# Attention's operations in another order, two weight tiles rounded behind it, other shares of dense work per step

## The chip, the cores and the metric

The kernel runs on one core of one Trainium2 chip. The metric is the device time of one execution in microseconds (us), the median of several runs. The engines are named as in the profile: PE (TensorE), DVE (VectorE), ACT (ScalarE), POOL (GpSimd), SP (SyncE, whose queue issues most DMAs).

## The reference

Three parts follow one another, all in float32 (the weights arrive as 64-bit words and are rounded on the chip):

```python
def _attn_ref(q, k, v):                      # batch 4, 8 heads, 576 positions, 64 wide
    scores = scale * np.matmul(q, k.transpose(0, 1, 3, 2))
    ...
    mask = (rel >= 0) & (rel < window)       # window 128
    scores = np.where(mask, scores + bias[None], -1000000000.0)
    scores = scores - np.max(scores, axis=-1, keepdims=True)
    attn = np.exp(scores)
    attn = attn / (np.sum(attn, axis=-1, keepdims=True) + 1e-09)
    return np.matmul(attn, v).astype(np.float32)

def _moe_ref(x, w_gate, w_val, w_out):       # 2304 tokens, 512 -> 1536 -> 512
    gate = 1.0 / (1.0 + np.exp(-(x @ w_gate)))
    val = x @ w_val
    return (gate * val @ w_out).astype(np.float32)

def _moe2_ref(x, w1, w2, w3, w_out):         # 512 -> 1024 -> 1024 -> 512
    h = (x @ w1) * (x @ w2) @ w3
    return (h @ w_out).astype(np.float32)
```

## The kernel before, in words

The 2304 tokens are 18 tiles of 128, in five blocks of 2, 4, 4, 4 and 4 tiles (`TILES`). A float32 product is made of three fast products (`PASSES`): every operand is split into a high part, rounded by ACT (`act_copy`, line 80), and a remainder, high subtracted from the value, by DVE (`dve_lo`, line 83) or POOL (`pool_lo`, line 86).

**Attention** goes in steps. There are 20 units n, five blocks by four head pairs (block n // 4, pair n % 4), and in step n the kernel traces three stages of different units: `stage_p(n-2)`, `stage_pv(n-3)` and `stage_s(n)` (`ORDER` changes that for the first seven steps).

- `stage_s` makes the scores on PE (line 730), 16 matmuls; then for each half (two tiles) DVE merges the two key windows (copy_predicated, 738), scales and adds the bias (741), reduces to the negated maximum (747, and 751 rescales it); ACT takes four exps with row sums (754); DVE adds 1e-9 and takes the reciprocal of the sums (757, 758); POOL scales two of the four (762) and ACT the other two (764).
- `stage_p` transposes on PE (772) into two PSUM banks, ACT copies each out (tile cp, line 80) and POOL cuts each into two masked halves (776, 780).
- `stage_pv` multiplies with V on PE (795) into one bank; ACT takes the high part (xth) and DVE the remainder (xtl), which is the last reader of the bank.

The four PSUM banks of tag "mm" are shared by the transposes, by pv and by all dense products of this part.

**Dense work beside attention.** The first expert layer's slices come in groups: groups 0 and 1 have one slice of 128, the later ones two. `layer(group, block)` makes gate and value products (`gv`, line 360, two products per slice, four pieces each, a piece being three matmuls), tanh on ACT (377), gate times value on DVE (384), its high part on ACT (line 80, tile gt) and remainder on POOL (line 86). The down products (`down1`, line 401, four pieces with one bank each) of a layer are traced behind the next layer's gv; DVE copies or adds each bank into `acc` (409, 411). `READY` says at which step a layer may begin. Behind the stages of a step `fill(FILL[n])` traces pieces until a budget is used up: a piece of a 512-wide layer is booked at 680, of the 256-wide block 0 at 360, and the last piece may overshoot. `FILL` has a default of 4000.

**Weights.** `convert_next` rounds the next weight tile of a queue: ACT takes an absolute value (146), DVE runs six operations (`rounded`, 147 to 152), then the tile is either split (ACT 80, POOL 86) into a weight slot `wsl`, or written to DRAM (`early32`) by a DMA of SP's queue, to be read back later as plain float32. `CONVERT` says how many tiles a step rounds. In attention these are three tiles each of groups 0 and 1 (gate, value, out), and six of group 2 (slices 2 and 3) that go to `early32`: (2,0), (3,0), (2,1), (3,1), (2,2), (3,2), where the second number is 0 for gate, 1 for value, 2 for out. Behind attention the tiles of group 2 are read back and split, and the tiles of later groups and of the second expert layer are rounded, all beside dense products.

**What sets the order.** PE's order in attention is the order of tracing (`manual_schedule`). Every other engine's order is fixed when the program is built, by a scheduler that takes the ready instruction of the best rank first; the rank is the place in the trace, moved ahead by `high_priority(offset=...)` of a positive offset and back by a negative one. On the chip each engine then runs its list strictly in order. Before the change attention's own operations carry no offset, dense evacuations have `SOONER` (150) and the rounding of weights has minus `LATER` (300).

Of the kernel before, what the change touches and what calls it, by code (L numbers as in the profile page):

```python
# [9 lines left out]
F32 = mybir.dt.float32  # L10
# [3 lines left out]
AF = mybir.ActivationFunctionType  # L14
ALU = mybir.AluOpType
AX = mybir.AxisListType
# [3 lines left out]
P = 128  # L20
# [10 lines left out]
PASSES = ((0, 0), (0, 1), (1, 0))  # L31
LATER = 300
SOONER = 150
FILL = {5: 0.0, 6: 1400.0, 7: 1400.0, 8: 0.0, 9: 0.0, 10: 2700.0, 11: 2700.0}
FULL = 4000.0

LAST_ORDER = (4, 0, 1, 2, 3)
# [19 lines left out]
def attn_moe_kernel(  # L57
# [14 lines left out]
    nc = tc.nc  # L72
# [6 lines left out]
    def act_copy(dst, src):  # L79
        return nc.scalar.activation(dst, src, AF.Copy)  # L80

    def dve_lo(dst, src, hi):
        nc.vector.tensor_tensor(dst, src, hi.bitcast(F32), ALU.subtract)  # L83

    def pool_lo(dst, src, hi):
        nc.gpsimd.tensor_tensor(dst, src, hi.bitcast(F32), ALU.subtract)  # L86
# [23 lines left out]


    spool = capool = None
    staged = {}
    rings = {"raw": 2, "raw32": 0, "ca": 2}
    held = {"raw": 0, "raw32": 0}
    queue = []
# [60 lines left out]
    groups = [(0,), (1,)] + [tuple(range(i, i + GF)) for i in range(GF, NF + NM, GF)]  # L177
# [116 lines left out]
    early = [it for it in fold_src if it[0][0] == "o2" or it[0][1] in W3_AHEAD]  # L294
# [2 lines left out]
    early += [((i, c), (w1, w2)[c][i - NF]) for i in groups[NF // GF + 2] for c in range(2)]  # L297
    early += [it for it in fold_src if it[0][0] == "w3" and it[0][1] in W3_LATER]
    late_n = len(early)
    early += [((i, c), (w_gate, w_val, w_out)[c][i]) for c in range(3) for i in groups[2]]  # L300
    early32 = dpool.tile([P * len(early), DM], F32, name="early32")
    ahead = {key: early32[i * P : (i + 1) * P, :] for i, (key, _) in enumerate(early)}
    ahead_items = [(("ahead", *key), src, None) for key, src in early]
# [45 lines left out]
    def gv(grp, blk, xs):  # L349

        pss = {}
        w = cols(blk)
        ns = w / 2.4 + 13.3

        def product(i, s):
            full = gvpool.tile([P, TB], F32, tag=gvtag, name=f"gv{i}_{blk}_{s}", bufs=gvbufs)
            ps = pss[i, s] = full[:, 0:w]
            for kk in range(NK):
                for wp, xp in PASSES:
                    nc.tensor.matmul(  # L360
                        ps,
                        wsl[i][:, s, wp, kk * P : (kk + 1) * P],
                        xs[blk][xp][:, kk],
                        start=(kk == 0 and wp == 0 and xp == 0),
                        stop=(kk == NK - 1 and wp == 1),
                    )
# [12 lines left out]
        for i in grp:  # L379
            yield from product(i, 1)  # L380
            pr = g[i]
            t = m2.tile([P, 2, TB], F32R, tag="gt", name=f"gt{i}_{blk}", bufs=4)[:, :, 0:w]
            with tc.high_priority(offset=SOONER):
                nc.vector.scalar_tensor_tensor(pr, pr, 1.0, pss[i, 1], ALU.add, ALU.mult)  # L384
                act_copy(t[:, 0], pr)
                pool_lo(t[:, 1], pr, t[:, 0])
            ts.append(t)
        return ts
# [218 lines left out]
    def attention(actx, conv):  # L607
# [108 lines left out]
        def stage_s(n):  # L716
            pair, blk, nt, t0, back = where(n)
            s, ld = st[n], loads[n]
            x = s["sm"] = ap2.tile([P, 4, 2, P], F32, tag="sm", name=f"sm{n}", bufs=3)
            up = 4.0**pair  # L720
            pss = {}
            for tp in range(nt // 2):
                side = (tp + n) % 2

                ps = pss[tp] = spsum.tile([P, 2, 2, 2, P], F32, tag=f"s{side}", name=f"s{n}_{tp}")
                for u in range(2):
                    t = 2 * tp + u
                    for h in range(2):
                        r = slice(D * h, D * h + D)
                        nc.tensor.matmul(  # L730
                            ps[:, h, :, u], ld["q"][r, t * P : (t + 1) * P], ld["k"][r, t * P : (t + 2) * P],
                            start=True, stop=True, skip_group_check=True,
                        )
            for tp in range(nt // 2):
                ps = pss[tp]
                g = slice(2 * tp, 2 * tp + 2)

                nc.vector.copy_predicated(  # L738
                    ps[:, :, 1], mask.unsqueeze(1).unsqueeze(1).broadcast_to([P, 2, 2, P]), ps[:, :, 0]
                )  # L740
                nc.vector.scalar_tensor_tensor(  # L741
                    x[:, g].rearrange("p g u k -> p g (u k)"), ps[:, :, 1].rearrange("p g u k -> p g (u k)"),
                    0.125 * up, tabs[blk][:, g].rearrange("p g u k -> p g (u k)"), ALU.mult, ALU.add,
                )
                mn = ap2.tile([P, 4], F32, tag="mn", name=f"mn{n}_{tp}", bufs=4)
                su = ap2.tile([P, 4], F32, tag="su", name=f"su{n}_{tp}", bufs=4)
                s["dve"] = nc.vector.tensor_reduce(  # L747
                    mn, x[:, g].rearrange("p g u k -> p (g u) k"), axis=AX.X, op=ALU.max, negate=True
                )
                if pair:  # L750
                    nc.vector.tensor_scalar(mn, mn, 1.0 / up, None, ALU.mult)  # L751
                for j in range(4):
                    y = x[:, 2 * tp + j // 2, j % 2]
                    s["act"] = nc.scalar.activation(  # L754
                        y, y, AF.Exp, bias=mn[:, j : j + 1], scale=1.0 / up, accum_out=su[:, j : j + 1]
                    )
                nc.vector.tensor_scalar(su, su, 1e-9, None, ALU.add)
                s["rec"] = nc.vector.reciprocal(su, su)  # L758
                for j in range(4):
                    y = x[:, 2 * tp + j // 2, j % 2]  # L760
                    if j < 2:
                        nc.gpsimd.tensor_scalar(y, y, su[:, j : j + 1], 1.0, ALU.mult, ALU.mult)  # L762
                    else:
                        nc.scalar.activation(y, y, AF.Copy, scale=su[:, j : j + 1])

        def stage_p(n):
            pair, blk, nt, t0, back = where(n)
            s = st[n]
            for h in range(2):
                ps = gvpool.tile([P, 4, P], F32, tag="mm", name=f"pt{n}_{h}")  # L770
                for t in range(nt):
                    nc.tensor.transpose(ps[:, t], s["sm"][:, t // 2 * 2 + h, t % 2], ident)  # L772
                cp = ap2.tile([P, 4, 2, P], F32, tag="cp", name=f"cp{n}_{h}", bufs=4)
                own, prev = cp[:, 0:nt, 1], cp[:, 0:nt, 0]
                act_copy(own, ps[:, 0:nt])
                nc.gpsimd.affine_select(
                    out=prev, in_=own, compare_op=ALU.is_gt, fill=0.0, base=0,
                    pattern=[[0, nt], [-1, P]], channel_multiplier=1,
                )
                s["pool"] = nc.gpsimd.affine_select(  # L780
                    out=own, in_=own, compare_op=ALU.is_ge, fill=0.0, base=0,
                    pattern=[[0, nt], [1, P]], channel_multiplier=-1,
                )
                s["cp", h] = cp.rearrange("p t c k -> p (t c k)")

        def stage_pv(n):
            pair, blk, nt, t0, back = where(n)
            s = st[n]
            ps = gvpool.tile([P, TB], F32, tag="mm", name=f"pv{n}")[:, 0 : nt * P]
            for j in range(-back, nt):  # L790
                a, b = max(j, 0) * P, min(j + 2, nt) * P
                m0 = 0 if j < 0 else (2 * j + 1) * P
                for h in range(2):
                    c = slice(h * D, (h + 1) * D)
                    nc.tensor.matmul(  # L795
                        ps[c, a:b], loads[n]["v"][:, j + 1, c], s["cp", h][:, m0 : m0 + b - a],
                        start=j == -back, stop=j == nt - 1, skip_group_check=True,
                    )
            if pair == 0:
                xt.append(x_tile("xt", blk))  # L800
            x = xt[blk]
            act_copy(x[0][:, pair], ps)
            dve_lo(x[1][:, pair], ps, x[0][:, pair])

        def fill(budget):

# [5 lines left out]
                    budget -= cost  # L812


        CONVERT = {1: 1, 3: 1, 5: 1, 8: 1, 9: 1, 10: 1, 11: 1, 12: 1, 13: 2, 14: 2}

        READY = {5: ((0, 0),), 10: ((0, 1),), 12: ((1, 0),), 14: ((0, 2), (1, 1)), 18: ((0, 3), (1, 2))}
        ORDER = {
# [57 lines left out]
    accpools.append(ctx.enter_context(tc.tile_pool(name="acc0", bufs=1)))  # L876
    with ExitStack() as conv, ExitStack() as actx:
        attention(actx, conv)


    rings.update({"raw": 3, "raw32": 4, "ca": 4})
# [158 lines left out]
```

## Time and profile before

| | |
|---|---|
| median of 3 runs | 909.33 us (908.82 to 909.49) |
| the profiled execution | 909.88 us |
| its span, first to last instruction | 908.2 us |
| PE busy | 872.8 us (96%) |
| PE's weight loads busy | 715.5 us (79%) |
| DVE busy | 661.1 us (73%) |
| ACT busy | 351.8 us (39%) |
| POOL busy | 313.3 us (35%) |
| mean granted clock of PE | 0.991 |

The profiled execution takes 1.68 us more than its span. The busy shares are averages over a kernel of several stages; attention lies in the first 187 us or so, where PE has nearly all of its idle time, and behind it PE is busy without a gap worth naming. A wait is put down to the event that came last before the waiting instruction.

### The profile page before, as it was taken

How to read it: one execution, taken by the hardware profiler on the slowest of the kernel's cores; microseconds unless marked ns; L12 is line 12 of the kernel's file. 1: busy time of each engine (PE TensorE's matmuls, PEld its weight loads, DVE VectorE, ACT ScalarE, POOL GpSimd, SP SyncE). 2: the span in 40 equal slices, each digit the busy share in tenths (PEclk: the TensorE clock that was granted, in tenths of full speed). 3: DMA queues.
4: the chain of work that ended last, by engine and by line, in shares of the span. 5: the costliest groups of instructions: out<-in, count | busy, mean ns of one | idle time of the engine just before them, and what ended most of it. 6: DMA issues, size and time to landing. Idle time of an engine off the chain costs nothing.

```text
span 908.2 us, 12508 instructions
## 1 busy us (share of the span) xinstructions
PE 872.8 (96%) x4432; PEld 715.5 (79%) x4432; DVE 661.1 (73%) x1156; ACT 351.8 (39%) x853; POOL 313.3 (35%) x352
## 2 busy tenths in 40 slices
PE   6789888999999999999999999999999999999998
PEld 4456666788888888888888888878788888888886
DVE  5978899579996995896599954396547886733444
ACT  6878576633322322322332343243433333222120
POOL 4666655543312412422431211103643551112121
PEclk9989999999999999999999999999999999999999
DMA  5444443144451251152054440128524445654322
GB/s 194 154 145 144 139 165 126 36 151 131 131 184 44 85 189 41 47 175 92 23 184 153 140 140 1 70 84 289 206 95 172 175 185 185 225 197 158 117 92 93
DMA packets 40623, 121.67 MB, mean 134 GB/s; under 512 B 4464, under 2 KB 6512, under 8 KB 38512
## 3 DMA queue, kind: packets, MB, share of 16 engines
q1 hardware_dynamic: 39264, 106.05, 35.0%
q10 hardware_dynamic: 1296, 14.81, 3.9%
q8 instruction: 35, 0.57, 0.3%
q14 instruction: 28, 0.23, 0.1%
HBM read 88.34 MB, written 32.51 MB: 133 GB/s over the span
## 4 chain that ended last, share of the span: by engine, by line
PE 80%; DVE 12%; ACT 3%; POOL 2%; issue 2%; DMA 0%; SPq 0%; ACTq 0%; DVEq 0%; POOLq 0%
PE gv L360 30%; PE dn L401 14%; PE o L591 11%; PE pb L472 9%; PE pd L472 4%; PE w3o L321 3%; PE lone L565 3%; PE pc L472 2%; PE pv L795 2%; DVE s L738 2%; ACT sm L754 2%; DVE sm L741 2%; DVE mn L747 1%; PE pt L772 1%; PE s L730 1%
## 5 line engine op out<-in xcount | busy, mean ns | idle before, releaser
L360 PE MATMUL gv<-xth,wsl 128*128 128x512 f32 (+1 forms) x960 | 281.5, 371 | 1.3 <-DVE acc L409 0.8
L360 PEld LDWEIGHTS gv<-xth,wsl 128*128 128x128 f32 x960 | 175.9, 190 | 35.7 <-issue 3.0
L360 PE MATMUL gv<-xtl,wsl 128*128 128x512 f32 (+1 forms) x480 | 177.8, 370 | 0.7 <-DVE xtl L83 0.7
L86 POOL TENSOR_TENSOR gt<-g,gt 128x512 fp32r<-128x512 f32 (+1 forms) x60 | 79.3, 1324 | 250.8 <-ACT gt L80 250.8
L401 PE MATMUL dn<-gt,wsl 128*128 128x512 f32 (+1 forms) x720 | 155.0, 369 | 8.4 <-DVE xtl L83 5.2
L401 PEld LDWEIGHTS dn<-gt,wsl 128*128 128x128 f32 x720 | 125.7, 188 | 33.1 <-issue 6.1
L360 PEld LDWEIGHTS gv<-xtl,wsl 128*128 128x128 f32 x480 | 91.2, 190 | 15.9 <-DVE xtl L83 1.3
L472 PE MATMUL pb<-xf,forms 128*128 128x512 f32 x384 | 97.7, 391 | 0.0
L411 DVE TENSOR_TENSOR acc<-acc,dn 128x512 f32<-128x512 f32 (+1 forms) x120 | 72.8, 626 | 16.9 <-PE dn L401 16.8
L472 PEld LDWEIGHTS pb<-xf,forms 128*128 128x128 f32 x384 | 70.8, 188 | 14.9 <-ACT xb L80 0.5
L384 DVE SCALAR_TENSOR_TENSOR g<-g,gv 128x512 f32<-128x512 f32 (+1 forms) x60 | 37.5, 628 | 52.8 <-PE gv L360 51.2
L80 ACT ACTIVATE gt<-g 128x512 fp32r<-128x512 f32 (+1 forms) x60 | 35.1, 586 | 76.2 <-DVE g L384 76.2
L754 ACT ACTIVATE sm<-sm,mn 128x128 f32<-128x128 f32 x144 | 55.8, 390 | 18.1 <-DVE mn L751 12.7
L601 DVE TENSOR_TENSOR acc<-acc,o 128x512 f32<-128x512 f32 x54 | 36.8, 683 | 32.8 <-PE o L591 32.7
L86 POOL TENSOR_TENSOR tp<-x,tp 128x512 fp32r<-128x512 f32 x16 | 21.4, 1338 | 86.3 <-ACT tp L80 86.2
L472 PE MATMUL pd<-xf,forms 128*128 128x512 f32 x192 | 48.9, 390 | 0.8 <-DVE xb L515 0.8
L377 ACT ACTIVATE g<-gv 128x512 f32<-128x512 f32 (+1 forms) x60 | 32.7, 548 | 41.1 <-PE gv L360 37.2
L591 PE MATMUL o<-outw,tp 128*128 128x512 f32 x192 | 48.0, 390 | 0.3 <-POOL tp L86 0.3
L591 PE MATMUL o<-outw,tq 128*128 128x512 f32 x192 | 48.2, 389 | 0.0
L762 POOL TENSOR_SCALAR sm<-sm,su 128x128 f32<-128x128 f32 x72 | 32.1, 458 | 42.2 <-DVE su L758 28.9
L321 PE MATMUL w3o<-wo,w3s 128*128 128x512 f32 x192 | 44.4, 390 | 0.4 <-ACT w3s L80 0.4
L795 PE MATMUL pv<-cp,ldv 128*64 128x256 f32 (+1 forms) x352 | 40.8, 373 | 3.2 <-POOL cp L780 3.2
(797 smaller groups left out, 1455.5 us busy)
## 6 DMA issues: line engine op xcount, KB each, us to landing
formd<-forms ACTq DMA_DIRECT2D x8, 1792.0 KB, 7.3
outw<-outd SPq DMA_DIRECT2D x16, 512.0 KB, 5.5
forms<-formd SPq DMA_DIRECT2D x8, 1024.0 KB, 5.2
ldk<-in_k_dram SPq DMA_DIRECT2D x16, 320.0 KB, 3.9
ldv<-in_v_dram SPq DMA_DIRECT2D x16, 320.0 KB, 3.1
out_dram<-acc SPq DMA_DIRECT2D x18, 256.0 KB, 2.0
ldq<-in_q_dram SPq DMA_DIRECT2D x16, 256.0 KB, 4.3
outd<-w3o SPq DMA_DIRECT2D x8, 512.0 KB, 2.9
```

What stands on the lines that cost most here:

```text
L80: return nc.scalar.activation(dst, src, AF.Copy)
L86: nc.gpsimd.tensor_tensor(dst, src, hi.bitcast(F32), ALU.subtract)
L321: nc.tensor.matmul(acc2, w3s[u][:, wp, i * P : (i + 1) * P], wo2[kk][:, xp], start=(kk == 0 and wp == 0 and xp == 0), stop=(kk == NC2 - 1 ...
L360: nc.tensor.matmul(ps, wsl[i][:, s, wp, kk * P : (kk + 1) * P], xs[blk][xp][:, kk], start=(kk == 0 and wp == 0 and xp == 0), stop=(kk == N ...
L384: nc.vector.scalar_tensor_tensor(pr, pr, 1.0, pss[i, 1], ALU.add, ALU.mult)
L401: nc.tensor.matmul(ps, wsl[i][:, 2, wp, m * P : (m + 1) * P], t[:, xp], start=n == 0, stop=n == 3 * len(grp) - 1,)
L411: nc.vector.tensor_tensor(a, a, ps, ALU.add)
L472: nc.tensor.matmul(ps, forms[i][:, a, wp, kk * P : (kk + 1) * P], xf[n, j][:, xp, kk], start=first and kk == 0 and (wp, xp) == PASSES[0], ...
L591: nc.tensor.matmul(ps, ts2[n, i][blk][:, xp, tt * P : (tt + 1) * P], outw[i][:, wp], start=k == 0, stop=k == 3 * len(grp) - 1,)
L601: nc.vector.tensor_tensor(a, a, ps, ALU.add)
L754: s["act"] = nc.scalar.activation(y, y, AF.Exp, bias=mn[:, j : j + 1], scale=1.0 / up, accum_out=su[:, j : j + 1])
L795: nc.tensor.matmul(ps[c, a:b], loads[n]["v"][:, j + 1, c], s["cp", h][:, m0 : m0 + b - a], start=j == -back, stop=j == nt - 1, skip_group_ ...
```

## The change

Nothing is computed otherwise. The table `RANKS` gives offsets to kinds of operations; a kind that is not in it gets 0. In effect three kinds are moved: the remainders xtl by +200, the exps of block 3 (units 12 to 15) by +200, and, while attention runs, the high part of the gate product from +150 to -100. The row sums `su` get eight buffers in place of four. The two out tiles of group 2, (2,2) and (3,2), are no longer among the tiles rounded in attention and written to `early32`: they are read as 64-bit words and rounded behind it. `CONVERT` spreads the ten tiles left over other steps, and `FILL` has other budgets.

```diff
-FILL = {5: 0.0, 6: 1400.0, 7: 1400.0, 8: 0.0, 9: 0.0, 10: 2700.0, 11: 2700.0}
+RANKS = {"xtl": 200, "gact": -100, ("exp", 3): 200}
+FILL = {5: 0.0, 6: 1400.0, 7: 2800.0, 8: 0.0, 9: 0.0, 10: 3400.0, 11: 3400.0, 12: 2600.0, 13: 2600.0, 16: 6100.0, 17: 4700.0, 18: 3300.0, 19: 6800.0}
...
+    def ranked(kind, n):
+
+        return tc.high_priority(offset=RANKS.get((kind, n // 4), RANKS.get(kind, 0)))
+
...
+    attending = [True]
...
-    early += [((i, c), (w_gate, w_val, w_out)[c][i]) for c in range(3) for i in groups[2]]
+    early += [((i, c), (w_gate, w_val, w_out)[c][i]) for c in range(2) for i in groups[2]]
...
             with tc.high_priority(offset=SOONER):
                 nc.vector.scalar_tensor_tensor(pr, pr, 1.0, pss[i, 1], ALU.add, ALU.mult)
+            with tc.high_priority(offset=RANKS["gact"] if attending[0] else SOONER):
                 act_copy(t[:, 0], pr)
+            with tc.high_priority(offset=SOONER):
                 pool_lo(t[:, 1], pr, t[:, 0])
...
-                su = ap2.tile([P, 4], F32, tag="su", name=f"su{n}_{tp}", bufs=4)
...
+                su = ap2.tile([P, 4], F32, tag="su", name=f"su{n}_{tp}", bufs=8)
...
+                with ranked("exp", n):
+                    for j in range(4):
+                        y = x[:, 2 * tp + j // 2, j % 2]
+                        s["act"] = nc.scalar.activation(
...
-            act_copy(x[0][:, pair], ps)
-            dve_lo(x[1][:, pair], ps, x[0][:, pair])
+            with ranked("xth", n):
+                act_copy(x[0][:, pair], ps)
+            with ranked("xtl", n):
+                dve_lo(x[1][:, pair], ps, x[0][:, pair])
...
-        CONVERT = {1: 1, 3: 1, 5: 1, 8: 1, 9: 1, 10: 1, 11: 1, 12: 1, 13: 2, 14: 2}
+        CONVERT = {1: 1, 3: 2, 8: 1, 10: 1, 11: 1, 12: 1, 13: 1, 14: 1, 7: 1}
...
         attention(actx, conv)
+    attending[0] = False
```

The other operations of the stages (kinds "cp", "st", "red", "rec", "scale", "ptc", "sel", "xth") are wrapped in the same way, with an offset of 0.

## Rows read from the trace of the kernel before

**Rows 1.** The page: busy time, share of the span, instructions.

```profile
PE 872.8 (96%) x4432; PEld 715.5 (79%) x4432; DVE 661.1 (73%) x1156; ACT 351.8 (39%) x853; POOL 313.3 (35%) x352
```

**Rows 2.** Windows: length; PE, PEld, DVE, ACT, POOL busy; clock; DMA.

```profile
20.00:40.00 20.00, 15.33 (x104) 10.52 (x102) 17.22 (x41) 14.85 (x56) 15.70 (x30) 1.00 0.62 198
45.00:65.00 20.00, 16.23 (x124) 11.68 (x120) 13.93 (x32) 15.07 (x54) 13.93 (x27) 0.88 0.48 151
70.00:80.00 10.00, 9.61 (x70) 7.24 (x72) 9.06 (x21) 8.60 (x34) 3.68 (x8) 0.99 0.48 152
...
80.00:155.00 75.00, 64.91 (x445) 49.57 (x442) 70.51 (x148) 49.80 (x173) 46.41 (x69) 0.95 0.45 152
155.00:170.00 15.00, 13.18 (x78) 9.51 (x78) 10.28 (x25) 10.76 (x44) 5.35 (x12) 1.00 0.10 28
176.00:194.00 18.00, 18.00 (x106) 14.00 (x106) 6.57 (x10) 7.32 (x14) 8.55 (x11) 1.00 0.35 109
...
194.00:280.00 86.00, 86.00 (x415) 72.65 (x414) 83.56 (x142) 27.17 (x48) 28.04 (x20) 1.00 0.47 152
```

**Rows 3.** Waits of PE, 80 to 155 us: us in total, times, longest.

```profile
PE dn L401 <- DVE xtl L83: 5.2, 2, 3.4
PE dn L401 <- DVE g L384: 2.1, 1, 2.1
PE pt L772 <- DVE acc L409: 1.4, 2, 0.9
PE gv L360 <- DVE acc L409: 0.8, 1, 0.8
```

**Rows 4.** Waits of PE, 20 to 80 us.

```profile
PE pt L772 <- POOL sm L762: 8.4, 6, 3.1
```

**Rows 5.** Chain of waits, 80 to 155 us: shares by engine and line.

```profile
by line: DVE sm L741 9.8%; DVE s L738 9.6%; issue 8.4%; DVE mn L747 7.6%; DVE acc L409 6.8%; ACT sm L754 6.3%; PE gv L360 6.1%; DVE xtl L83 4.9%; DVE su L757 4.2%; DVE g L384 2.1%; DVE mn L751 2.1%; DVE su L758 2.0%; DVE s_('ahead', 3, 2)_1
```

**Rows 6.** Timeline of DVE, rounding of (0,2), (2,2), (3,2): start, us, what.

```profile
40.56 0.39 DVE L147 TENSOR_SCALAR a_(0, 2)_456<-a_(0, 2)_456 128x512 f32<-128x512 f32 x1
...
43.95 0.74 DVE L152 TENSOR_TENSOR a_(0, 2)_456<-a_(0, 2)_456,s_(0, 2)_457 128x512 f32<-128x512 f32 x1
...
131.86 0.76 DVE L147 TENSOR_SCALAR a_('ahead', 2, 2)_1439<-a_('ahead', 2, 2)_1439 128x512 f32<-128x512 f32 x1
...
139.02 0.41 DVE L150 TENSOR_SCALAR s_('ahead', 2, 2)_1440<-a_('ahead', 2, 2)_1439 128x512 uint32<-128x512 uint32 x1
...
140.66 0.69 DVE L152 TENSOR_TENSOR a_('ahead', 2, 2)_1439<-a_('ahead', 2, 2)_1439,s_('ahead', 2, 2)_1440 128x512 f32<-128x512 f32 x1
...
141.96 0.39 DVE L147 TENSOR_SCALAR a_('ahead', 3, 2)_1449<-a_('ahead', 3, 2)_1449 128x512 f32<-128x512 f32 x1
...
143.77 1.40 DVE L150 TENSOR_SCALAR s_('ahead', 3, 2)_1450<-a_('ahead', 3, 2)_1449 128x512 uint32<-128x512 uint32 x1
...
145.98 0.74 DVE L152 TENSOR_TENSOR a_('ahead', 3, 2)_1449<-a_('ahead', 3, 2)_1449,s_('ahead', 3, 2)_1450 128x512 f32<-128x512 f32 x1
```

**Rows 7.** Timeline of POOL: a remainder at 37.76, one at 143.17, one at 197.92.

```profile
37.76 1.27 POOL L86 TENSOR_TENSOR wsl<-a_(0, 1)_298,wsl 128x512 fp32r<-128x512 f32 x1
...
143.17 1.71 POOL L86 TENSOR_TENSOR gt<-g,gt 128x512 fp32r<-128x512 f32 x1
...
197.92 1.74 POOL L86 TENSOR_TENSOR wsl<-raw_(3, 2)_2161,wsl 128x512 fp32r<-128x512 f32 x1
```

**Rows 8.** Timelines of ACT, DVE and PE: the wait at 92.71, in its order.

```profile
88.76 0.57 ACT L80 ACTIVATE xth<-pv 128x512 fp32r<-128x512 f32 x1
...
91.89 0.68 DVE L83 TENSOR_TENSOR xtl<-pv,xth 128x512 fp32r<-128x512 f32 x1
...
92.71 0.59 PE L401 MATMUL dn<-gt,wsl 128*128 128x256 f32 x3 [3.41 <-DVE xtl L83]
```

**Rows 9.** Groups of ACT, 20 to 170 us: the exps.

```profile
L754 ACT ACTIVATE sm<-sm,mn 128x128 f32<-128x128 f32 x124 | 48.1, 390 | 12.4 <-DVE mn L751 10.8 <-DVE mn L747 1.2
```

**Rows 10.** Timeline of PE: the first down product of group 2.

```profile
230.92 3.04 PE L401 MATMUL dn<-gt,wsl 128*128 128x256 f32 x24
```

More of the change, by code (lines that the diff above doesn't have):

```diff
@@ L736, in stage_s @@
                 g = slice(2 * tp, 2 * tp + 2)
[L738 to L744, printed above, removed]
-                mn = ap2.tile([P, 4], F32, tag="mn", name=f"mn{n}_{tp}", bufs=4)
@@ L746, in stage_s @@
-                su = ap2.tile([P, 4], F32, tag="su", name=f"su{n}_{tp}", bufs=4)
[L747 to L755, printed above, removed]
-                    )
@@ L757, in stage_s @@
[L757 to L764, printed above, removed]
+                with ranked("cp", n):
+                    nc.vector.copy_predicated(
+                        ps[:, :, 1], mask.unsqueeze(1).unsqueeze(1).broadcast_to([P, 2, 2, P]), ps[:, :, 0]
+                    )
@@ new lines, in stage_s @@
+                with ranked("st", n):
+                    nc.vector.scalar_tensor_tensor(
+                        x[:, g].rearrange("p g u k -> p g (u k)"), ps[:, :, 1].rearrange("p g u k -> p g (u k)"),
+                        0.125 * up, tabs[blk][:, g].rearrange("p g u k -> p g (u k)"), ALU.mult, ALU.add,
+                    )
+                mn = ap2.tile([P, 4], F32, tag="mn", name=f"mn{n}_{tp}", bufs=4)
+                su = ap2.tile([P, 4], F32, tag="su", name=f"su{n}_{tp}", bufs=8)
@@ new lines, in stage_s @@
+                with ranked("red", n):
+                    s["dve"] = nc.vector.tensor_reduce(
+                        mn, x[:, g].rearrange("p g u k -> p (g u) k"), axis=AX.X, op=ALU.max, negate=True
+                    )
+                    if pair:
+                        nc.vector.tensor_scalar(mn, mn, 1.0 / up, None, ALU.mult)
+                with ranked("exp", n):
+                    for j in range(4):
+                        y = x[:, 2 * tp + j // 2, j % 2]
+                        s["act"] = nc.scalar.activation(
+                            y, y, AF.Exp, bias=mn[:, j : j + 1], scale=1.0 / up, accum_out=su[:, j : j + 1]
+                        )
@@ new lines, in stage_s @@
+                with ranked("rec", n):
+                    nc.vector.tensor_scalar(su, su, 1e-9, None, ALU.add)
+                    s["rec"] = nc.vector.reciprocal(su, su)
+                with ranked("scale", n):
+                    for j in range(4):
+                        y = x[:, 2 * tp + j // 2, j % 2]
+                        if j < 2:
+                            nc.gpsimd.tensor_scalar(y, y, su[:, j : j + 1], 1.0, ALU.mult, ALU.mult)
+                        else:
+                            nc.scalar.activation(y, y, AF.Copy, scale=su[:, j : j + 1])
@@ L774, in stage_p @@
                 own, prev = cp[:, 0:nt, 1], cp[:, 0:nt, 0]
[L775 to L783, printed above, removed]
+                with ranked("ptc", n):
+                    act_copy(own, ps[:, 0:nt])
+                with ranked("sel", n):
+                    nc.gpsimd.affine_select(
+                        out=prev, in_=own, compare_op=ALU.is_gt, fill=0.0, base=0,
+                        pattern=[[0, nt], [-1, P]], channel_multiplier=1,
+                    )
+                    s["pool"] = nc.gpsimd.affine_select(
+                        out=own, in_=own, compare_op=ALU.is_ge, fill=0.0, base=0,
+                        pattern=[[0, nt], [1, P]], channel_multiplier=-1,
+                    )
                 s["cp", h] = cp.rearrange("p t c k -> p (t c k)")
```

## The prediction, made before the changed kernel ran

> **What bounds the kernel now.** The busy shares come first [rows 1]: PE works 96% of the span, DVE 73%. Taken alone that leaves PE some 35 us (908.2 - 872.8). The windows by stage show where these lie [rows 2]: from 194 to 280 us PE is busy without a gap, from 80 to 155 us it is busy 64.9 of 75 us, at a mean granted clock of 0.95. In that stretch DVE is busy 70.5 us, 94%. PE's waits there [rows 3] end on DVE almost without exception: 5.2 us on the remainder xtl, 2.1 us on the gate product g, 1.4 and 0.8 us on the copies to acc. The chain of waits [rows 5] says the same from the other side: it runs over DVE's mask merge, bias, maximum and acc, and the last entry printed is a rounding operation of tile (3,2), so the rounding of weights, ranked last, sits on the path. Earlier it is otherwise: from 20 to 80 us PE waits 8.4 us for POOL's scaling of the softmax [rows 4], the latency of one unit's chain through DVE, ACT and POOL, with DVE busy 17.2 of 20 us and later 13.9 of 20 [rows 2].
>
> So attention from 80 to 155 us is bound by DVE, before that by latency, and all behind it by PE. The ceiling of a gain from 80 to 155 us is what PE loses there: 10.1 us idle (75 - 64.9), and 3.75 us to the clock (0.05 of 75; half speed is the 1.2 GHz level of the two), 13.8 us in all.
>
> **Two tiles rounded behind attention.** This takes (2,2) and (3,2) out of steps 13 and 14. Of the six DVE operations of each, the first and last stand in [rows 6], with the fourth. Those of (3,2) take 0.39, 0.42, 0.74, 1.40, 0.74 and 0.74, sum 4.4 us; those of (2,2) sum to 3.8 us. Together 8.2 us of DVE's 70.5. One ACT operation, one write of 256 KB on SP's queue and one on its way back go with each. If DVE keeps its present 4.5 us of idle time (75 - 70.5), the stretch becomes 70.5 - 8.2 + 4.5 = 66.8 us, 8.2 less. PE needs 64.9 - 3.75 = 61.2 us at full clock for the same work, so it fits. The bounds are 0 (other work takes the place) and 12.7 (DVE at 62.3 without a gap). I take 8.2, because operations of both tiles stand on the chain without a gap on DVE before them.
>
> Within this sum one operation deserves a look: L150 took 1.40 us for (3,2) and 0.41 for (2,2) [rows 6], and the long one ran while POOL made a two-input remainder from 143.17 for 1.71 us [rows 7]; their ends are 0.3 us apart. The Trainium skill (SBUF — State Buffer, "SBUF: two separate sides") says that DVE and GpSimd share a port pair, that a DVE operation in a two-port mode or a two-input GpSimd operation locks it whole, and that the other blocks. By that rule the 1.0 us is POOL's and would fall on another DVE operation, and this term would be 7.2 instead of 8.2. The sum below does not use it.
>
> Behind attention the same operations return. DVE is busy 6.6 of 18 us from 176 to 194 us [rows 2], so there are 11.4 us free for 8.2. Today the last remainder of these tiles ends at 199.7 [rows 7] and the first down product that reads them starts at 230.9 [rows 10]: 31 us of cover, for at most 8.2 us of rounding and the larger read. The rounding of later tiles slips by as much; DVE is 97% busy from 194 to 280 us, yet PE does not wait there. Cost 0, high bound 1 us (the DVE evacuations queued behind a rounding operation of up to 1.4 us).
>
> **The rounding moved between steps.** (0,2) goes from step 5 to 3, (1,0) from 8 to 7, (1,1) from 9 to 8; (3,1) from 13 to 14. The six operations of (0,2) sum to 3.3 us, first and last in [rows 6]. From 20 to 40 us DVE has 2.8 us free, POOL 4.3 for the remainder of 1.27 us [rows 2, 7]. What does not fit, 0.5 us, delays a chain for which PE already waits. Bounds: 0, and 3.3 + 1.3 = 4.6. I take 0.5, the windows being of that stretch. From 45 to 65 us DVE has 6.1 us free, more than one tile; 0, at most 3.3.
>
> **xtl at +200.** The wait at 92.71 shows the pattern [rows 8]: pv's high part ran on ACT at 88.76, its remainder only at 91.89, since DVE was working off other operations, and the fourth down product waited 3.41 us for the bank that xtl reads last. Ahead of the others, xtl could have begun at 89.3, 2.6 us sooner. But where DVE is the bound, another operation is later by the same 0.6 us. Bounds: 0, and all 5.2 us [rows 3]. I take 1.0, nearer to 0, since the rows of DVE show no idle time to win, only PE's order to suit.
>
> **The rest.** The gate product's high part at -100: the down products of a layer come a whole layer later, so the copy may be later; 0. Exps of block 3 first: 0 in the forecast; priced as a rival. Eight su buffers: 0, they only remove waits. FILL: a piece overshoots, and layers have a first step, so some budgets change nothing: step 7 has only four pieces left, as before, and step 17 has one left. By the kernel's own booking (0.68 a piece, 0.36 in block 0) step 10 gets 0.7 us more dense work and step 11 0.8, step 12 1.4 less, steps 16 and 17 +2.0 and -2.0, steps 18 to 21 -0.7, +2.7, 0 and -2.0. All pieces are done by the same end. In step 12 the four down products of 92.71 are gone to step 11, where fewer tiles are being rounded; there PE is busy 96% already [rows 2], so the added 1.4 us may lengthen 70 to 87 us and give it back behind. 0, at most +1.4. From 155 to 170 us PE idles 1.8 us [rows 2], which I leave.
>
> **Sum.** -8.2 + 0.5 - 1.0 = -8.7 us. The profiled execution took 909.88 us, 1.68 more than its span, and stands 0.55 above the median of 909.33; against itself it would be 901.2, against the median **900.6 us**.
>
> **The rivals.**
>
> *All of the loss goes.* If rank and lighter DVE together end PE's waits, the clock stays up too: -13.8, and -1.8 behind it: 909.3 - 15.6 = 893.7 us. For it: the three levers meet in the same stretch. Against: DVE would have to run at 100%. Chance 0.15, from 893.7 to 897.
>
> *Given back early.* The tile moved to step 3 costs 4.6 and those of steps 7 and 8 3.3: 900.6 + 4.1 + 3.3 = 908. For it: PE already waits there for that chain [rows 4]. Against: the free time in the windows. Chance 0.13, from 905 to 909.
>
> *PE is the bound anyway.* Then what DVE gives up is worth nothing, the dense pieces only change places, and the time is 909.3. For it: 96% against 73% [rows 1]. Against: the waits of [rows 3] are real idle time of PE. Chance 0.07. The Trainium skill (Perfetto Trace Analysis, "Identifying the Most-Contended Engine") would have one optimize the engine with the highest occupancy first, which over the whole span would be PE; the windows of this trace say that it is DVE in this stretch.
>
> *Slower.* Block 3's exps at +200 pass the high part xth of pv in steps 12 to 15. A unit has eight, of 0.39 us each [rows 9]: 3.1 us. ACT must do xth before DVE can do xtl, whatever xtl's rank, so the bank comes free 3.1 us later and the wait of [rows 8] returns in each of the four steps: 4 x 3.1 = 12.4, and 900.6 + 12.4 = 913 us; with today's 3.75 us lost to the clock on top, 917. It decides where xth starts more than about 3 us after pv's end. For it: the bank is what the down product waits for today [rows 8]. Against: PE does s and three down products before it needs the bank. Chance 0.15.
>
> **How the numbers follow.** The forecast has 0.50, with its own range 897 to 905. A measurement of this kernel can tell about 0.2% from no change: 907.5 to 911.1. Faster: 0.50 + 0.15 + 0.09 of the early case = 0.74. Same: 0.07 + the other 0.04 = 0.11. Slower: 0.15. The range from 893.5 to 910.5 holds all but the slower case.
>
> **What would show it.** Right: from some 80 us to the last score of attention about 8 us shorter; no "dn waits for xtl" of more than a microsecond; twelve DVE operations of (2,2) and (3,2) behind attention with PE at 100%. PE's wait for POOL's scaling before 80 us stays at 8 to 10 us. Wrong: that wait grows past 12 us (early case); xth more than 3 us behind pv in steps 12 to 15 and PE waiting on it (slower); or DVE's idle time in the stretch growing by 8 us while its length stays (PE or latency the bound).

## The result, and the profile after

The changed kernel takes **900.6 us** (median of 4 runs, 898.9 to 901.1) against 909.4 (908.8 to 910.3) for the one before, measured side by side: the ratio is 0.9899, 95% interval 0.9882 to 0.9916, so 8.8 us less. The profiled execution has a span of 899.4 us, 8.8 less than before.

The page's busy times, which answer to [rows 1]:

```profile
PE 867.7 (96%) x4432; PEld 711.5 (79%) x4432; DVE 657.8 (73%) x1156; ACT 351.3 (39%) x853; POOL 309.7 (34%) x352
```

The shares are those of before, to a per cent. What moved shows only by place. PE does the score products s of one unit per step, so the start of each s gives a clock of steps in every trace. In the table, "step n" starts with its s; "last pv" is the start of the last value product of attention. Starts are taken to a tenth, so a difference can be off by 0.1.

| stretch | before, us | after, us | difference |
|---|---|---|---|
| 0 to step 12 | 86.0 | 85.4 | -0.6 |
| step 12 to step 19 | 77.2 | 66.3 | -10.9 |
| step 19 to last pv | 21.9 | 21.8 | -0.1 |
| last pv to the end of the span | 723.2 | 725.9 | +2.7 |

So attention ended 11.5 us sooner, and 2.7 of these were lost again behind it. Now the two traces in the long stretch, steps 12 to 19. Windows of the kernel before (length; then PE, PEld, DVE, ACT, POOL busy, granted clock, DMA share, GB/s):

```profile
86.00:163.20 77.20, 66.42 (x451) 50.47 (x448) 70.23 (x151) 51.52 (x186) 43.46 (x67) 0.96 0.39 131
```

and of the changed kernel, in the same columns:

```profile
85.40:151.70 66.30, 60.94 (x433) 45.96 (x431) 58.70 (x132) 48.21 (x179) 36.05 (x63) 1.00 0.41 129
```

PE's idle time fell from 10.8 us (77.2 - 66.42) to 5.4. Its clock went from a mean of 0.96 to 1.00, worth some 3.1 us (0.04 of 77.2, an estimate). By the kernel's own booking the new FILL puts 2.1 us of dense work elsewhere (1.44 into steps 10 and 11, 0.68 behind step 19). 5.4 + 3.1 + 2.1 = 10.6 of the 10.9. The waits of PE that are left, steps 12 to 19 of the changed kernel (us in total, times, longest):

```profile
PE dn L410 <- DVE xtl L84: 1.3, 1, 1.3
PE dn L410 <- DVE g L391: 1.0, 1, 1.0
PE pv L812 <- ACT g L384: 1.0, 2, 0.7
PE pt L787 <- POOL sm L777: 0.8, 2, 0.5
PE gv L367 <- DVE xtl L84: 0.4, 1, 0.4
PE s L739 <- PE pv L812: 0.4, 1, 0.4
PE pt L787 <- DVE acc L418: 0.3, 1, 0.3
```

Of the waits of [rows 3], those for xtl fell from 5.2 to 1.3 us and those of pt for acc from 1.4 to 0.3. And the chain of waits from 85 to 152 us, which answers to [rows 5]:

```profile
by line: ACT sm L767 18.1%; PE pv L812 8.6%; PE gv L367 8.5%; DVE s L748 8.1%; DVE sm L752 6.8%; DVE mn L759 6.5%; DVE xtl L84 4.8%; PE s L739 4.5%; DVE acc L418 4.5%; issue 4.0%; PE dn L410 4.0%; ACT sm L779 3.3%; ACT xth L81 3.1%; PE pt L
```

It no longer begins with DVE: ACT's exps lead, and PE's own products come next, though the DVE lines shown still add up to 31%. From 20 to 80 us PE waits 7.7 us for POOL's scaling, 9 times, against the 8.4 of [rows 4]: that part is as it was.

All this looks like the prediction come true. The runs say otherwise about the reason.

### The profile page after: what moved, and what is told of

The parts are those of the page before. It is cut to its first block, busy times and chain, and to the rows that moved or that the text cites. A ratio compares the mean times of both kernels' runs of the same rounds, so it can differ in the third digit from the quotient of the medians.

```text
span 899.4 us, 12474 instructions
## 1 busy us (share of the span) xinstructions
PE 867.7 (96%) x4432; PEld 711.5 (79%) x4432; DVE 657.8 (73%) x1156; ACT 351.3 (39%) x853; POOL 309.7 (34%) x352
## 4 chain that ended last, share of the span: by engine, by line
PE 71%; DVE 17%; ACT 5%; DMA 3%; issue 3%; POOL 2%; DVEq 0%; ACTq 0%; POOLq 0%; SPq 0%
PE gv L367 24%; PE dn L410 12%; PE o L600 11%; PE pb L481 9%; PE pd L481 4%; PE w3o L328 3%; ACT sm L767 2%; PE pv L812 2%; PE pc L481 2%; PE lone L574 2%; DVE s L748 2%; DMA raw_(15, 1)_5897<-early 1%; DVE sm L752 1%; DVE mn L759 1%; DVE acc L420 1%
## 5 line engine op out<-in xcount | busy, mean ns | idle before, releaser
L87 POOL TENSOR_TENSOR gt<-g,gt 128x512 fp32r<-128x512 f32 (+1 forms) x60 | 76.6, 1280 | 242.4 <-ACT gt L81 242.4
L767 ACT ACTIVATE sm<-sm,mn 128x128 f32<-128x128 f32 x144 | 55.9, 390 | 19.3 <-DVE mn L763 11.9
L481 PEld LDWEIGHTS pd<-xf,forms 128*128 128x128 f32 x192 | 36.0, 188 | 8.5 <-DVE xa L540 1.0
```

What stands on the lines that cost most here:

```text
L481: nc.tensor.matmul(ps, forms[i][:, a, wp, kk * P : (kk + 1) * P], xf[n, j][:, xp, kk], start=first and kk == 0 and (wp, xp) == PASSES[0], ...
L767: s["act"] = nc.scalar.activation(y, y, AF.Exp, bias=mn[:, j : j + 1], scale=1.0 / up, accum_out=su[:, j : j + 1])
```

## The experiments

Three levers stand in the change: the two **tiles** (2,2) and (3,2) behind attention, the **ranks**, and the new **FILL**. The moved steps for rounding are a fourth, which the prediction had priced at 0.5 us; no kernel has them alone, nor the eight su buffers, which stand in every kernel made from the changed one and in e2. Each kernel was timed in five rounds beside the kernel before on its chip; differences are between these medians.

| kernel | us | before | difference | ratio, 95% |
|---|---|---|---|---|
| e1 tiles alone, old steps | 909.15 | 909.23 | -0.1 | 0.9997 (0.9985 to 1.0009) |
| e2 ranks alone, with the su buffers | 904.98 | 909.23 | -4.3 | 0.9953 (0.9935 to 0.9970) |
| e3 FILL alone | 909.65 | 909.23 | +0.4 | 1.0013 (0.9999 to 1.0027) |
| f1 tiles, FILL, new steps (no ranks) | 903.59 | 909.80 | -6.2 | 0.9931 (0.9917 to 0.9945) |
| f2 tiles, ranks, new steps (no FILL) | 906.77 | 909.80 | -3.0 | 0.9963 (0.9951 to 0.9974) |
| f3 ranks, FILL (no tiles, old steps) | 906.34 | 909.80 | -3.5 | 0.9960 (0.9948 to 0.9972) |
| e5 all but xtl's rank | 902.78 | 909.80 | -7.0 | 0.9915 (0.9900 to 0.9930) |
| e8 all, old steps | 904.09 | 910.12 | -6.0 | 0.9924 (0.9903 to 0.9946) |
| g1 tiles, FILL of steps 16 to 19 only | 906.43 | 910.12 | -3.7 | 0.9959 (0.9943 to 0.9975) |
| h1 all, a third tile behind | 901.46 | 910.12 | -8.7 | 0.9902 (0.9885 to 0.9919) |
| h2 all, one tile from step 14 to 5 | 906.15 | 910.12 | -4.0 | 0.9950 (0.9933 to 0.9967) |
| e4 all, the two tiles not rounded | 899.67 | 909.23 | -9.6 | 0.9894 (0.9874 to 0.9914) |

### The two tiles alone (e1)

```diff
-early += [... for c in range(3) for i in groups[2]]
+early += [... for c in range(2) for i in groups[2]]
-CONVERT = {..., 13: 2, 14: 2}
+CONVERT = {..., 13: 1, 14: 1}
```

> The kernel before with one part of the change: the tiles (2,2) and (3,2) are rounded behind attention (one tile each in steps 13 and 14), all ranks, budgets and other steps as before. Theory (DVE's load is the bound from step 12 to the last score): those 8.2 us of DVE lie on the chain, so 909.4 falls by 7 to 9, to 900.5 to 902.5, and the last score starts 7 to 9 us earlier than 163.2. Rival (the order of the lists is what counts, the waits for xtl and g are behind the loss): at most 4 us, 905.5 or more, and PE still waits some 5 us for xtl. Second rival (what is rounded behind attention costs as much there): 907 or more with PE waiting behind 190 us.

Measured: no gain, -0.1 us. The prediction's largest term, 8.2 us, is not there. Window of this kernel, steps 12 to 19:

```profile
84.30:160.80 76.50, 66.89 (x452) 50.67 (x448) 64.28 (x139) 50.06 (x184) 40.77 (x67) 0.93 0.34 112
```

DVE does 5.95 us less (64.28 against 70.23), the stretch is 0.7 us shorter, and DVE's idle time grows from 7.0 to 12.2 us. That is the sign that the prediction had named for "wrong". Two things explain it. First the place: PE's longest wait for xtl is there as before, 3.39 us at 91.01, because in step 12 neither tile is being rounded. Second, where they were rounded, in steps 15 to 17, PE had little to lose. The timeline of PE in the kernel before, step 17:

```profile
148.07 0.93 PE L401 MATMUL dn<-gt,wsl 128*128 128x512 f32 x3 [1.76 <-DVE xtl L83]
149.86 1.16 PE L772 MATMUL pt<-ident,sm 128*128 128x128 f32 x8 [0.86 <-DVE acc L409]
```

These two, 2.6 us, are all that PE waits from 130 to 154 us, where the two tiles are rounded. And in e1 one of them grew in the place of the other; PE, then DVE, of e1:

```profile
147.15 1.53 PE L772 MATMUL pt<-ident,sm 128*128 128x128 f32 x8 [2.37 <-DVE acc L409]
148.61 3.22 PE L795 MATMUL pv<-cp,ldv 128*64 128x128 f32 x20
```

```profile
143.07 0.69 DVE L83 TENSOR_TENSOR xtl<-pv,xth 128x512 fp32r<-128x512 f32 x1 [1.79 <-ACT xth L80]
...
146.32 2.47 DVE L409 COPY acc<-dn 128x512 f32<-128x512 f32 x4
```

The four down products of step 17 hold PSUM banks until acc is copied, and pt wants a bank. DVE stands idle 1.79 us ahead of xtl, waiting for ACT's xth, and then does mask, bias and maximum of the next unit before acc. After PE's wait the clock falls (a mean of 0.60 from 148.6 to 151.9 us): the pv at 148.61 takes 3.22 us, where the others of this form take 1.95. As these rows read, the bound was a sequence of bank, ACT, DVE and bank, not the sum of DVE's work; no kernel with more banks was run to try it.

### The ranks alone (e2)

```diff
+RANKS = {"xtl": 200, "gact": -100, ("exp", 3): 200}
-su = ap2.tile([P, 4], F32, tag="su", ..., bufs=4)
+su = ap2.tile([P, 4], F32, tag="su", ..., bufs=8)
```

> The change without its tiles, steps and budgets: only the three ranks and the eight su buffers on the kernel before. Theory (load): the same DVE work in another order, so 0 to 2 us less, 907.5 to 909.4. Rival (order): 4 us or more less, 905.4 or below, with the wait of down products for xtl (5.2 us before) gone. If it is slower, the ranks need the lighter DVE to pay.

Measured: -4.3 us, where the prediction had 1.0 for xtl and nothing for the other two ranks. Steps 12 to 19, and PE's waits for xtl in them:

```profile
84.50:157.10 72.60, 65.67 (x448) 50.46 (x446) 65.10 (x147) 49.87 (x184) 40.81 (x65) 0.95 0.42 140
```

```profile
PE dn L410 <- DVE xtl L84: 2.1, 3, 1.2
```

That is 72.6 us instead of 77.2, and 2.1 us of waits instead of 5.2. Which of the three ranks does it was not tried by itself. No wait of PE for xth appears in steps 12 to 15.

### FILL alone (e3)

```diff
-FILL = {5: 0.0, 6: 1400.0, 7: 1400.0, 8: 0.0, 9: 0.0, 10: 2700.0, 11: 2700.0}
+FILL = {..., 10: 3400.0, 11: 3400.0, 12: 2600.0, 13: 2600.0, 16: 6100.0, 17: 4700.0, ...}
```

> The kernel before with the new budgets per step alone. Theory (load): dense work changes places by at most 2.7 us a step, DVE keeps its load, so within 1.5 us of 909.4. Rival (the spread of PE's work is a lever of its own, since steps 10 and 11 take work out of the stretch that DVE binds): 2 us or more less, 907.4 or below.

Measured: +0.4 us, not told from nothing. That is the theory's range, but not for its reason: steps 12 and 13 became 3.1 us shorter (20.8 against 23.9, 1.44 of it moved elsewhere), but steps 16 and 17 grew from 19.8 to 24.2 us. FILL moves three of step 17's four down products into step 16. PE there, in e3:

```profile
135.92 2.20 PE L401 MATMUL dn<-gt,wsl 128*128 128x512 f32 x9
...
140.50 0.63 PE L772 MATMUL pt<-ident,sm 128*128 128x128 f32 x4 [2.38 <-DVE su L758]
142.97 1.12 PE L772 MATMUL pt<-ident,sm 128*128 128x128 f32 x4 [1.84 <-ACT cp L80]
144.78 3.68 PE L795 MATMUL pv<-cp,ldv 128*64 128x128 f32 x20 [0.69 <-ACT cp L80]
```

4.9 us of waits, and a pv of 3.68 us instead of 1.95 (the mean clock from 144.7 to 148.6 us is 0.53). The pt is that of unit 15. The profile puts its wait down to su, the last thing that DVE finished before it, but that reciprocal belongs to unit 16; unit 15's scaling was done by 135.5. What pt lacks, by the rows, is a bank: three of the four hold the down products until acc is copied, and the fourth the value product until DVE has made g. DVE was rounding first:

```profile
132.58 0.77 DVE L149 SCALAR_TENSOR_TENSOR a_('ahead', 2, 2)_1439<-raw_('ahead', 2, 2)_1318,a_('ahead', 2, 2)_1439 128x512 uint32<-128x512 uint32 x1
...
133.78 0.68 DVE L738 COPY_PREDICATED s<-mask,s 128x512 f32<-128x512 int32 x1
...
139.68 0.68 DVE L384 SCALAR_TENSOR_TENSOR g<-g,gv 128x512 f32<-128x512 f32 x1
140.28 0.17 DVE L758 RECIPROCAL su<-su 128x4 f32<-128x4 f32 x1
...
145.01 1.87 DVE L409 COPY acc<-dn 128x512 f32<-128x512 f32 x3
```

Step 16's s starts at 129.78; the mask merge that follows it comes 4.0 us later, g 9.9 us and acc 15.2 us later. Between, from 129.77 to 139.7 us, DVE runs nine rounding operations, 5.7 us by their records.

So alone the three levers give -0.1, -4.3 and +0.4, together -3.9; the whole gave -8.8. Some 4.9 us come from parts meeting, or from the moved steps, which are in the whole and in none of the three; e8 below has the three without them. The next four kernels each leave one part out.

### Leaving one out (f1, f2, f3, e5)

```diff
f1: -RANKS = {"xtl": 200, "gact": -100, ("exp", 3): 200}
    +RANKS = {"gact": SOONER}
f2: the old FILL
f3: range(3) and the old CONVERT
e5: +RANKS = {"gact": -100, ("exp", 3): 200}
```

> The changed kernel with every rank taken back (gact at SOONER as before, xtl and the exps at 0); the two tiles behind attention, the new steps for rounding and the new FILL stay. The parts alone gave 0 (two tiles), -4.3 (ranks) and +0.4 us (FILL), together -3.9 where the whole gave -8.8: 4.9 us must come from parts meeting. Theory, the cycle of the PSUM banks: the free DVE time of the two tiles and the emptier steps 12 and 17 pay only where the remainder xtl and the exps may use them, so without ranks little is left, 907 (905.5 to 909.5), with dn waiting for xtl over 3 us in all between steps 12 and 19. Rival, FILL unlocks the tiles: FILL alone lost because two tiles are rounded in steps 14 to 16 where it books most work; with the tiles gone it pays by itself, and this kernel keeps the 4.9 us: 904.5 (903.5 to 905.5), with no wait of dn for xtl above 2 us.

> The changed kernel with the old FILL; ranks, the two tiles and the new steps for rounding stay. Theory, the cycle of the banks: ranks and free DVE time meet in xtl, FILL only trims, so most of the gain is here, 902 (900.5 to 903.5). Rival, FILL unlocks the tiles: what meets is FILL and the tiles, so without FILL only the ranks' gain is left, 905 (904 to 906), with step 17's four down products again the longest step.

> The changed kernel with the two tiles (2,2) and (3,2) rounded in attention as before, and rounding in its old steps; ranks and FILL stay. Both theories say that the tiles are one of the two that meet: 905 (904 to 906), the ranks' gain alone, with the waits of pt for DVE and ACT in steps 14 to 17 that FILL alone showed (2.4 us on su, 1.8 on cp). A third reading, that ranks and FILL meet and the tiles are worth nothing in any company: 901 (900 to 902).

> The changed kernel with xtl at rank 0; the gate copy's and the exps' ranks stay. By the cycle of the banks xtl is the rank that counts, as the bank that dn waits for comes free with it: 905 (903.5 to 907), with dn waiting for xtl 3 to 6 us between steps 12 and 19 (1.3 in the changed kernel). Rival, the exps of block 3 and the late gate copy do it on ACT, where xth stood behind both: 901 (900 to 902).

My theory that xtl's rank makes the free DVE time usable fell: without any rank 6.2 us of the gain remain (expected 2.3), without FILL 3.0 (expected about 7), and without xtl's rank alone 7.0 (expected 4.3), with dn waiting for xtl 1.7 us there, not 3 to 6. The rival was the better one: **FILL and the tiles unlock each other**. It holds in number for f1 (903.6 of 903.5 to 905.5); f2 (906.8) and f3 (906.3) lie a little above its 904 to 906, so by the medians tiles and ranks, or ranks and FILL, give no more than the ranks alone. In f3 pt waits 2.6 us for ACT's cp. f1, f2 and e5 have the moved steps too; g1 below is without them. PE in steps 16 and 17 of f1, with FILL and a single rounding operation left there:

```profile
133.05 2.21 PE L410 MATMUL dn<-gt,wsl 128*128 128x512 f32 x9
135.10 1.03 PE L787 MATMUL pt<-ident,sm 128*128 128x128 f32 x8
136.29 1.95 PE L812 MATMUL pv<-cp,ldv 128*64 128x128 f32 x20 [0.16 <-DVE acc L418]
...
140.10 0.96 PE L410 MATMUL dn<-gt,wsl 128*128 128x512 f32 x3
```

and DVE beside it:

```profile
133.67 0.66 DVE L391 SCALAR_TENSOR_TENSOR g<-g,gv 128x512 f32<-128x512 f32 x1
134.24 0.68 DVE L418 COPY acc<-dn 128x512 f32<-128x512 f32 x1
```

The same products as in e3, with 0.16 us of waits instead of 4.9: g is done 0.8 us before pt, and the first bank of dn comes free at 134.9. The steps, from the profiled executions:

| | step 12 to 14 | step 16 to 18 | step 12 to 19 |
|---|---|---|---|
| before | 23.9 | 19.8 | 77.2 |
| tiles (e1) | 24.2 | 21.7 | 76.5 |
| FILL (e3) | 20.8 | 24.2 | 75.5 |
| ranks (e2) | 20.8 | 21.1 | 72.6 |
| ranks, FILL (f3) | 19.3 | 22.2 | 71.7 |
| tiles, ranks (f2) | 22.7 | 17.8 | 71.9 |
| tiles, FILL (f1) | 18.9 | 16.9 | 67.2 |
| all | 18.8 | 16.7 | 66.3 |

In steps 16 and 17 the tiles alone cost 1.9 us and FILL alone 4.4; both gain 2.9. The tiles and the ranks gain 2.0 there without FILL (f2). In steps 12 and 13 FILL or the ranks each take away most of the wait of [rows 8] (FILL by putting the down products elsewhere; the ranks in e2, but not in f2); both together gain 1.5 us more (f3), and beside the tiles FILL alone has nearly all of it (f1). With FILL and the tiles in place the ranks are worth 0.9 us in the whole stretch; by the medians they are worth 2.6, the rest of it outside.

### The place (g1) and the moved steps (e8)

```diff
g1: e1, with FILL = {old..., 16: 6100.0, 17: 4700.0, 18: 3300.0, 19: 6800.0}
e8: CONVERT = {1: 1, 3: 1, 5: 1, 8: 1, 9: 1, 10: 1, 11: 1, 12: 1, 13: 1, 14: 1}
```

> The kernel before with the two tiles behind attention (rounding in its old steps) and, of the new FILL, only the budgets of steps 16 to 19; no ranks. Theory: FILL and the tiles meet in one place, steps 16 and 17. From the start of stage_s of step 16 to that of step 18 the runs so far took 19.8 us before, 21.7 with the tiles alone, 24.2 with FILL alone, 16.9 with both. So this stretch should take 16.5 to 18 us here while steps 12 and 13 keep their 24 us, and the time be 905 (903.5 to 906.5). Rival: the two need the budgets of steps 10 to 13 as well, or the new steps for rounding, so the stretch is above 19 us and the time 908.5 to 909.5.

g1's windows, steps 16 and 17:

```profile
129.30:146.90 17.60, 17.06 (x123) 12.80 (x120) 15.23 (x29) 12.21 (x44) 11.58 (x21) 1.00 0.40 120
```

17.6 us against 21.7 with the tiles alone, while steps 12 and 13 keep their 23.9; the time falls by 3.7 us (906.4, within the 903.5 to 906.5 expected, at its upper end). Ranks, su buffers and moved steps are as before in g1. So the place is shown: FILL and the tiles meet in steps 16 and 17, and need nothing else for it.

> The changed kernel with rounding in its old steps (one tile in step 5 instead of the second in 3, one in 9 instead of 7), the two tiles still behind attention, ranks and FILL as changed. The prediction had 0.5 us lost by that move. If it holds: 900 (899.5 to 900.5). If the moves do something in steps 7 to 9, where the changed kernel waits less for POOL's scaling than the one before: 902 (901 to 904).

904.1, just above the upper of the two ranges. Steps 12 to 19 take 66.4 us, as in the changed kernel; what differs lies ahead of it (step 12 starts at 88.5 instead of 85.4). But e8's own executions run from 899.96 to 906.03 us, and its interval overlaps with the changed kernel's: that the moved steps gain some 2 to 3 us is likely, not settled. By e8 the three levers give -6.0 together, against -3.9 as a sum, so by the medians 2.1 of the 4.9 us come from their meeting and 2.8 go with the moved steps. In steps 12 to 19 the traces give some 4 us to the meeting (10.8 less together; 0.7, 4.6 and 1.7 apart). What differs between executions of one kernel in the early steps stays open.

### More of the same (h1, h2), and the price behind (e4)

```diff
h1: +early += [...][:-1]        # (3,1) too is rounded behind attention
    CONVERT without step 14
h2: CONVERT: step 14's tile in step 5
```

> The changed kernel with a third tile, (3,1), rounded behind attention as well. With PE's waits gone, DVE is busy 42.5 of 43 us from 84 to 127 us in the changed kernel: there it now is the bound, and the tile's 3.6 us of DVE in step 14 should come out of steps 14 to 16: 3 us less to the last pv, some 0.5 to 1 given back behind, so 898 (897 to 899.5). Rival, order and banks bound it even so, and one more tile behind attention costs there what it gains: 900.5 to 902.

> The changed kernel with one tile more rounded in step 5 and none in step 14, so that every later tile is rounded a step or two sooner. DVE is busy 98% from 84 to 127 us and some 80% from 33 to 58 us: if DVE's load is now the bound of the former, 898 (896.5 to 899.5). Rival: in step 5 it delays the chain of the softmax for which PE waits (1.5 us at 38.1, 1.7 at 40.5), and gives back what it gains: 900.5 to 903.

Both theories miss: h1 (901.5) falls into its rival's range, and h2 (906.2) lies above its rival's 903. In the changed kernel DVE is idle for only 0.9 of the 43 us from 84 to 127 us (it is busy 42.1, not the 42.5 that I wrote), and I again took this for a bound. h1's window, steps 12 to 19:

```profile
87.20:153.50 66.30, 60.90 (x433) 45.72 (x431) 56.29 (x126) 47.61 (x177) 35.39 (x63) 1.00 0.38 117
```

2.4 us less work for DVE, and the stretch is 66.3 us to the tenth. h2 has 66.5 there and loses ahead of it (step 12 at 89.6; waits for POOL's scaling 10.3 us, longest 3.0). Neither beats the changed kernel.

e4 reads the two tiles' values from other data, already rounded, and so leaves out their rounding behind attention; the true out weights of slices 2 and 3 never enter.

```diff
+if i in groups[2] and c == 2:
+    return ahead[i, 0]
```

> The changed kernel with work left out: the out tiles of slices 2 and 3 are not rounded at all, their place is taken by the gate tiles that already lie rounded in DRAM, read a second time. So what the two tiles cost behind attention is missing. Theory: behind attention the changed kernel lost 2.7 us against the kernel before, half of it at one wait of gv for the gate product near 264 us, because DVE's rounding is later by the two tiles; here that wait is gone and the time is 1.2 to 2.7 us below the changed kernel's 900.6, 898 to 899.4. Rival (those waits come from where the order happens to fall, not from the two tiles): within 0.5 us of 900.6.

899.7, between the two expectations and 0.9 us below the changed kernel's median, and the intervals overlap. From the last pv to the end of the span it takes 724.2 us, 1.7 less than the changed kernel, but still 1.0 more than the kernel before: the price of rounding the two tiles there lies between nothing and some 2 us, and a part of the 2.7 is not theirs. The four kernels that round them in attention (before, e2, e3, f3) lie between 723.0 and 723.6 there, the nine that round them behind it between 724.3 (g1) and 727.5 (f1). One place can be seen in the changed kernel, first DVE, then POOL, then PE:

```profile
261.20 1.79 DVE L156 SCALAR_TENSOR_TENSOR a_(7, 0)_3166<-raw_(7, 0)_3042,a_(7, 0)_3166 128x512 uint32<-128x512 uint32 x1
...
263.58 0.68 DVE L391 SCALAR_TENSOR_TENSOR g<-g,gv 128x512 f32<-128x512 f32 x1
```

```profile
261.09 1.35 POOL L87 TENSOR_TENSOR gt<-g,gt 128x512 fp32r<-128x512 f32 x1 [13.54 <-ACT gt L81]
```

```profile
264.31 0.50 PE L367 MATMUL gv<-xth,wsl 128*128 128x512 f32 x1 [0.89 <-DVE g L391]
```

The rounding of later tiles has slipped (this L156 starts 87.7 us behind the last pv; its like 77.4 in the kernel before and 76.9 in e4, where it takes 0.68 us), one of its operations runs long beside POOL, and the gate product behind it is late for PE by 0.89 us, some 70 us after the two tiles themselves. In e4 PE waits nowhere for as much as 0.2 us between 174 and 300 us. Another 0.9 us or so (0.8 us of waits before, 1.1 + 0.6 after) come near 643 us, at the start of the second half; some of the kernels with the tiles behind show it and some do not, and its cause was not tried.

## Why the prediction was right in number and wrong in its reason

- **The time**, 900.6, was met; the terms behind it were not.
- **Two tiles, -8.2**: the step that failed is "attention from 80 to 155 us is bound by DVE". Alone they give -0.1 (e1), and a third tile gives nothing (h1). A busy share of 91% from step 12 to 19 (94% in the window of the prediction) contained operations that nobody waited for, and the saved work was subtracted from a 75 us window although it all lay in some 15 us of it (131.9 to 146.7). DVE's busy time fell by 5.95 us besides, not by 8.2. What I had given as the reason, operations of both tiles on the chain of [rows 5], is a place, not a price. The trace had the better bound: 2.6 us of waits of PE in the stretch where the two are rounded. In company with FILL the tiles are needed (e8's -6.0 against f3's -3.5, both with the old steps), but for their place, not for their sum. The Trainium skill (Perfetto Trace Analysis, "Identifying the Most-Contended Engine") has one optimize the engine of highest occupancy first; within steps 12 to 19 that is DVE (70.2 us; PE's weight loads, one of the two measures that the page has for PE, 50.5). Here the measurement differs: lightening DVE takes 0.7 us off that stretch in e1 and nothing in h1.
- **The 1.0 us of a blocked operation** inside that term could not matter, the term itself being nothing. The pairing itself came back: in e3 the same L150 of tile (3,2) took 1.37 us at 142.17, while POOL's remainder ran from 141.56 for 1.69.
- **xtl at +200, -1.0**: right sign, mis-sized. The ranks alone gave -4.3, near the upper bound of 5.2; how much of it is xtl's was not run. I had priced them as a reordering on a full engine; since DVE was not the bound, nothing else had to pay. In company they give 2.6 (-8.8 against f1's -6.2), of which xtl some 1.8 (e5's -7.0, whose interval overlaps with that of the whole). The rank is no guarantee: f2 has it, and PE still waits 3.04 us for xtl at 90.33, in step 12.
- **FILL, 0**: wrong in kind. Nothing alone, in company the largest part of the gain: 5.8 us between f2 and the whole, and 3.6 between e1 and g1 from the budgets of steps 16 to 19 alone. I had checked what each budget adds to a step, but not what DVE does in step 16 while the three moved down products hold banks.
- **Moved rounding, +0.5**: more likely a gain of 2 to 3 (e8), unsettled.
- **Behind attention, 0, bound 1**: the trace shows +2.7 from the last pv on. The slip of later tiles, for which I had put nothing, costs 0.89 us near 264 us, a wait that is gone in e4. The 1.0 us that e4 keeps are not the rounding's and stay open, so the bound of 1 for the tiles is neither borne out nor refuted.
- **What would show it**: the score products of steps 11 to 19 span 75.6 us instead of 84.8, and the two tiles are rounded between 183.2 and 195.2 us with PE at 100%, both as foreseen. A wait for xtl over a microsecond was to be gone; one is left. It is the course of events that "slower" described: the eight exps of unit 12 run on ACT from 92.8 to 95.9 us, then cp and the scaling, and xth starts 4.0 us behind pv's end, at 98.0; xtl follows at 98.6 and PE's down product at 99.5. But f1, which has no ranks, has xth 3.7 us late at the same place and a wait of 1.0 us. So the delay exists, once, and the exps' rank is not what makes it.
- **The rivals**: "PE is the bound anyway" found nothing for it, "slower" only the wait just named. "All of the loss goes" came nearest in mechanism: the clock did return to 1.00, as it said, though 5.4 us of idle time stayed and 2.7 were lost behind.

That a sum of wrong terms met the median is luck: the two tiles' -8.2 came to nothing alone, and about as much came from terms put at nothing or near it, FILL beside the tiles, the ranks and, likely, the moved steps.

## What to carry to other kernels

Price a saving by the waits at the very place where the saved work runs, not by the busy share of a window around it: 5.95 us less work for an engine that was 91% busy left the time as it was. The waits hold for the present order only, and are read again when the load beside them changes. Where a schedule is written out by hand, the load of a step and the work that another engine does beside it have to be changed together: each alone cost 2 to 4 us in steps 16 and 17, both gained 3. And test parts in pairs as well as alone, and each part once: here three parts summed to -3.9 and were -6.0 together, and a fourth that was never run alone stood in the -8.8.

## What the runs showed that I had not expected

- A short idle time of PE can cost twice. In e1 and in e3 the pv behind waits of 2.4 and 4.9 us took 3.22 and 3.68 us instead of 1.95, at mean clocks of 0.60 and 0.53, where 0.5 is the lower of the two levels (1.2 GHz); the mean of steps 12 to 19 was 0.93 in both, and 1.00 in the changed kernel, whose longest wait there is 1.3. Not every wait does it: the 1.76 and 0.86 us of the kernel before at 148 and 150 us left its pv at 1.95.
- The cost of a DVE operation depends on its neighbour. L156 takes 0.68 us by itself and took 1.79 beside POOL's remainder at 261.09; both ended within 0.6 us of each other, and the 1.1 us more are about what was left of POOL's operation when L156 began (1.2). The Trainium skill (SBUF — State Buffer, "SBUF: two separate sides") says that DVE and GpSimd share a port pair that one of them locks for a whole instruction; the rows agree with that.
- Executions of one kernel can differ by more than the effect sought: e8's six lie between 899.96 and 906.03 us on one chip. A difference of 2 us between two single traces is then no evidence by itself, and only differences seen in several kernels (steps 12 to 19: 66.3 to 67.2 us in each of the seven kernels that have all of FILL and neither tile rounded in attention) should carry an argument; what rests above on one trace, such as the 1.0 us of e4, is weaker.
